# Attention beside an MLP on one core: the order of v products, dense products and scores within a unit of TensorE work

## The chip, the cores and the metric

The kernel runs on one core of one Trainium2 chip. The metric is the device time in microseconds of one execution. Before the change it is 1629.68 us, the median of three runs (1628.3 to 1630.91).

## What is computed

The reference, cut to its core (S = 2048 rows, D = 512, 32 heads of 16, F = 1792):

```python
xn = _layernorm(x)
# attention
q, k, v = heads((xn @ wqkv))                   # 32 heads, 16 wide
scores = einsum("bhqd,bhkd->bhqk", q, k) * 16 ** -0.5
o = einsum("bhqk,bhkd->bhqd", softmax(scores), v)
# MLP
h = gelu(xn @ w1 + b1)
out = x + o @ wo + (h @ w2 + b2)
```

All inputs and the output are float32.

## The kernel before, in words

Operands of the dense products and of the scores are split into two float16 parts, and a product is made of three float16 products. TensorE is used as two row halves of 64 rows, each with four column groups of 32. `tiled` (line 177) issues one product of a half as four matmuls, one for each column group, so one product fills a half. The two halves hold different work at the same time; what a half does is called its side, 0 or 1.

Three kinds of work share TensorE. The scores are made twice: as S (`s_half`, line 224, tile pS), whose row maxima VectorE takes with a reduction (line 236), and, 20 units later and transposed, as T (`e_half`, line 269, tile pT), which ScalarE turns into exponentials (line 283, tile pe) with the maxima already subtracted in the product. One S and one T stand together in the order and are called a pair here (`scores`, line 582). The products with v (`v_one`, line 299, tile pV, float32) take the exponentials of earlier units; a round is four of them, one for each head and column group. The dense products (tile pD) belong to the MLP, to the later projections of q and k, and to the output product; they come in groups (`Group`, line 394) that gather in one PSUM bank and are then evicted. A generator hands the groups over one at a time, and `dense(gen, side, n)` (line 546) issues up to n products of the current group on one side; it stops where the group has none left for that side. A group ends when both sides are done.

The order on TensorE is written out by hand in `unit` (line 562); the engines' queues keep it. One unit makes four pairs on side r (r changes from unit to unit), two rounds with v on side 1-r (`v_turn`, a generator that yields behind each round), and dense products on both sides. How many is the group's `pace`: a pair of numbers, for side 1-r and side r. The first dense product of the MLP (w1, evicted by `hidden`, 24 products a group, 14 groups to a block of 512 rows) alternates (4, 4) and (3, 3); the second (w2, 84 products a group, four groups a block) has (3, 3) in blocks 0 and 1 and (3, 4) in blocks 2 and 3; projections and output have (4, 4).

PSUM has eight banks: at any time three for S, three for T, one for the dense group and one for the products with v. A group that ends gives its bank to T's list and the next takes T's oldest. An S must wait until the reduction that read its bank has ended, a T for the exponential. Because both halves add into one bank, a v product or a dense product that changes side waits until the last one of the other side has ended (`product`, line 159).

VectorE also evicts w1's groups (line 969), ScalarE evicts w2's groups and takes the tanh (lines 984 and 939), and GpSimdE does the rest of the gelu in small steps that `tick` hands out unit by unit. DMAs are issued on SyncE.

Of the kernel before, what the change touches and what calls it, by code (L numbers as in the profile page):

```python
# [24 lines left out]
NC = D // P  # L25
# [3 lines left out]
NG = H // 4  # L29
VW = DH + 1  # L30
LEAD = 20
FAST, MEAN, SLOW = (4, 4), (3, 4), (3, 3)
MEASURE = (3, 0, 1, 2)
POOL_NS = 2500
TAIL = 5
# [11 lines left out]
def layer_kernel(ctx: ExitStack, tc: tile.TileContext, x, wqkv, wo, w1, b1, w2, b2, out):  # L47
# [104 lines left out]
    PAIRS = ((0, 0), (0, 1), (1, 0))  # L152
# [37 lines left out]
    def later(n, fn, local=False):  # L190
        queue.append((slot[0] + n, fn, local))
# [10 lines left out]
    def pooled(*todo):  # L202
        steps.extend(todo)
# [8 lines left out]
    def tick():  # L212
        run_due()
        run_steps()
        slot[0] += 1
# [8 lines left out]
    def s_half(u, n):  # L224

        t, i = divmod(u, 16)
        g, qb = divmod(t, NQB)
        qt, kb = divmod(i, 4) if t else (i % 4, i // 4)
        if t not in mt_of:
            mt_of[t] = work.tile([P, 4, 4, 4], F32, name="mt", bufs=2)  # L230
        ks, qs = kst[g % 2], qst[g % 2]
        p, a = divmod(n, 2)
        r = slice(64 * a, 64 * a + 62)
        s = banks("S")
        tiled(None, a, s, qs[p][qb][r, qt * P:(qt + 1) * P], ks[p][kb][r, :], True, True)
        nc.vector.reduce_max(mt_of[t][:, n, qt, kb:kb + 1], s, axis=AX.X)  # L236
# [283 lines left out]
    pos, spent, cur = [0], [False], [None]  # L520

    def group(gen):

        if cur[0] is None and not spent[0]:
            cur[0] = next(gen, 0)
            if cur[0] == 0:
                cur[0], spent[0] = None, True
        return cur[0]

    def ended():  # L530

        if cur[0] is not None and cur[0].over():
            done, cur[0] = cur[0], None
            newest.pop("D", None)
            done.end()

    def burst(gen, n):

        while n > 0 and (f := group(gen)) is not None:
            if not f.usable():  # L540
                break
            f.product(2)
            n -= 1
            ended()

    def dense(gen, side, n):

        while n > 0 and (f := group(gen)) is not None and f.usable(side):
            f.product(side)
            n -= 1  # L550
            ended()
# [10 lines left out]
    def unit(gen):  # L562

        u = pos[0]
        e = u - LEAD
        if e < 0:
            pos[0] += 1
            for n in range(4):  # L570
                s_half(u, n)
            s_end(u)
            burst(gen, LFILL[u - 16])
            tick()
            return
        if e == 0 and cur[0] is not None:
            burst(gen, cur[0].left())
        r = e % 2

        v = v_turn(1 - r, pos[0] - (2 if e < NU else 0))  # L580

        def scores(i):
            k, n = divmod(i, 2)
            if u - r < NU:
                s_half(u - r + k, 2 * n + r)
            if e - r < NU:
                e_half(e - r + k, 2 * n + r)

        pace = cur[0].pace if cur[0] is not None else FAST
        dense(gen, 1 - r, pace[0] - 2)  # L590
        scores(0)
        dense(gen, 1 - r, 2)
        scores(1)
        next(v, None)
        scores(2)
        next(v, None)
        scores(3)
        for _ in v:
            pass
        dense(gen, r, pace[1])  # L600
        for t in [t for t in pv_of if summed[t] == [32] * 4]:
            v_end(t)
        for key in [k for k in ptiles if not any(w[1:] == k for side in due for w in side)]:
            del ptiles[key]
        pos[0] += 1
        if u < NU and r:
            s_end(u)
        tick()
# [9 lines left out]
    with ExitStack() as st1:  # L618
# [285 lines left out]
        while not spent[0] or more or cur[0] is not None:  # L904
            unit(fil)
            if pos[0] > 16:
                more = next(pre, 0) != 0
# [3 lines left out]
    def mlp():  # L911
        m2 = st2p
        w2_s = m2.tile([P, 2, NF, D], F16, name="w2_s")
        b2_b = m2.tile([P, D], F32, name="b2_b")
        xbs, wcs = {}, {}

        def fetch_x(b):
            if b < NQB:
                xbs[b] = m2.tile([P, 2, NC, QB], F16, name="xb", bufs=1)
                nc.sync.dma_start(xbs[b], xn_d[:, :, :, b * QB:(b + 1) * QB])  # L920

        def fetch_w1(n):
            if n < NQB * NF:
                wcs[n] = m2.tile([P, 2, NC, P], F16, name="wc", bufs=3)
                nc.sync.dma_start(wcs[n], w1_d[n % NF])

        fetch_x(0)
        for n in range(2):
            fetch_w1(n)
        for _ in range(8):  # L930
            yield None

        done = set()

        def gelu(hh, g, b, f):
            t1 = m2.tile([P, QB], F32, name="t1", bufs=2)

            def tanh():
                nc.scalar.activation(t1, t1, AF.Tanh, scale=GELU_C * GELU_A)
                later(1, rest, True)  # L940

            def rest():
                pooled((690, lambda: nc.gpsimd.tensor_scalar(t1, t1, 1.0, gs[:, 1:2], op0=ALU.add, op1=ALU.mult)),
                       (1280, lambda: nc.gpsimd.tensor_tensor(t1, t1, hh, op=ALU.mult)),  # L944
                       (620, lambda: nc.gpsimd.tensor_scalar(g[:, 0, f, :], t1, 1.0, 0.0, op0=ALU.mult, op1=ALU.add)),
                       (1160, lambda: nc.gpsimd.tensor_tensor(g[:, 1, f, :], t1, g[:, 0, f, :], op=ALU.subtract)),  # L946
                       (0, lambda: done.add((b, f))))

            pooled((1040, lambda: nc.gpsimd.tensor_tensor(t1, hh, hh, op=ALU.mult)),  # L949
                   (620, lambda: nc.gpsimd.tensor_scalar(t1, t1, 1.0, 1.0 / GELU_A, op0=ALU.mult, op1=ALU.add)),  # L950
                   (1280, lambda: nc.gpsimd.tensor_tensor(t1, t1, hh, op=ALU.mult)),  # L951
                   (0, lambda: later(2, tanh, True)))

        for b in range(NQB):
            xb = xbs[b]
            g = m2.tile([P, 2, NF, QB], F16, name="g", bufs=1)
            for f in range(NF):
                fetch_w1(b * NF + f + 2)
                wc = wcs[b * NF + f]
                if b == 0 and f >= 3:  # L960
                    nc.sync.dma_start(w2_s[:, :, f - 3:NF if f == NF - 1 else f - 2, :],
                                      w2_d[:, :, f - 3:NF if f == NF - 1 else f - 2, :])
                if b == 0 and f == 3:
                    nc.sync.dma_start(b2_b, b2[None, :].to_broadcast([P, D]))

                def hidden(hp, g=g, b=b, f=f):
                    hh = m2.tile([P, QB], F32, name="hh", bufs=3)
                    scale, bias = fac1[0][:, f // 2:f // 2 + 1], b1_s[:, f:f + 1]
                    nc.vector.tensor_scalar(hh, hp, scale, bias, op0=ALU.mult, op1=ALU.add)  # L969
                    later(1, lambda: gelu(hh, g, b, f), True)  # L970

                yield Group([lambda c=c, i=i, j=j, wc=wc, xb=xb: (wc[:, i, c, :], xb[:, j, c, :])
                             for c in range(NC) for i, j in PAIRS], dbank, hidden, pace=FAST if f % 2 else SLOW)
            for q in range(4):
                t = b * 4 + q
                xa = m2.tile([P, D], F32, name="xa", bufs=2)
                if q == 1:
                    fetch_x(b + 1)
                nc.sync.dma_start(xa, x[t * P:(t + 1) * P, :])
                later(3, lambda xa=xa: pooled((1280, lambda: nc.gpsimd.tensor_tensor(xa, xa, b2_b, op=ALU.add))), True)  # L980

                def store(yp, xa=xa, t=t):
                    yt = m2.tile([P, D], F32, name="yt", bufs=2)
                    nc.scalar.activation(yt, yp, AF.Copy, scale=gs[:, 2:3])  # L984
                    add = lambda: nc.gpsimd.tensor_tensor(xa, xa, yt, op=ALU.add)  # L985
                    put = lambda: nc.sync.dma_start(acc_d[t * P:(t + 1) * P, :], xa)
                    later(1, lambda: pooled((1280, add), (0, lambda: later(1, put, True))), True)

                yield Group([lambda f=f, i=i, j=j, q=q, g=g: (g[:, i, f, q * P:(q + 1) * P], w2_s[:, j, f, :])
                             for f in range(NF) for i, j in PAIRS], dbank, store,  # L990
                            lambda n, b=b: (b, n // 3) in done, pace=SLOW if b < 2 else MEAN)
# [128 lines left out]
```

## Time and profile before

| | before |
|---|---|
| median of 3 runs | 1629.68 us (1628.3 to 1630.91) |
| the profiled execution | 1630.98 us, its span 1629.1 us |
| granted TensorE clock | 0.992 |
| TensorE busy | 97% of the span, 38915 matmuls |
| VectorE, ScalarE, GpSimdE busy | 88%, 85%, 41% |
| reductions of S (line 236) | 2048, mean 683 ns |
| exponentials (line 283) | 2048, mean 688 ns |

A line of the profile names the source line, engine and operation, the tiles written and read, the shape of one instruction and the count; then the busy time, the mean duration of one, and the idle time of that engine just before, with what ended it. All tiled products carry the line of `product` (161), so they are told apart by tile: pS, pT, pV, pD. In the timeline the first two columns are the start and the length of a row of equal instructions that follow each other. The lengths of matmuls are modelled and overlap, so the distance between starts is what a product costs.

### The profile page before, as it was taken

Reading aid. Unit: us, or ns where it says so; the run is one execution under the profiler, and the core shown is the slowest. Engines: PE = TensorE matmul, PEld = TensorE weight load, DVE = VectorE, ACT = ScalarE, POOL = GpSimd, SP = SyncE. Lnnn points to the kernel's source line nnn. Section 1 sums busy time; section 2 is a strip of 40 time slices with the busy share of each in tenths; the row PEclk is TensorE's granted clock in tenths of the full one; section 3 lists DMA queues with packets and bytes.
Section 4 is the critical chain, followed back from the end, with each engine's and each line's share of the span. In section 5 each row is a group of like instructions: output and inputs, shape, how many; then the busy total and the mean of one; then the engine's idle time right before and its main releaser. Section 6 shows DMA issues by size and latency. Waiting matters only on the chain.

```text
span 1629.1 us, 85743 instructions
## 1 busy us (share of the span) xinstructions
PE 1583.1 (97%) x38915; PEld 965.3 (59%) x38915; DVE 1425.7 (88%) x2388; ACT 1383.9 (85%) x2254; POOL 668.5 (41%) x742
## 2 busy tenths in 40 slices
PE   8987999979999999999999999999999999999998
PEld 3434666636666666666566666666666656665554
DVE  8887988869999999999999999999999989998901
ACT  4316988869999999999999999999999989998893
POOL 3112686527774110677412166761117774111000
PEclk9999999989999999999999999999999999999999
DMA  6475475451112111211111111221111100004122
GB/s 201 145 229 174 115 191 171 133 187 45 44 42 62 41 40 38 60 50 38 51 37 50 41 45 39 58 62 39 39 48 49 40 27 25 26 23 146 54 87 99
DMA packets 120934, 125.79 MB, mean 77 GB/s; under 512 B 39036, under 2 KB 90620, under 8 KB 120440
## 3 DMA queue, kind: packets, MB, share of 16 engines
q1 hardware_dynamic: 120568, 120.30, 25.2%
q8 instruction: 304, 4.98, 1.3%
q14 instruction: 62, 0.51, 0.1%
HBM read 81.79 MB, written 38.39 MB: 74 GB/s over the span
## 4 chain that ended last, share of the span: by engine, by line
PE 84%; DVE 5%; DMA 4%; POOL 3%; SPq 1%; issue 1%; ACT 1%; POOLq 0%; DVEq 0%; ACTq 0%
PE pV L161 29%; PE pD L161 26%; PE pS L161 13%; PE pT L161 11%; DVE mt L236 3%; PE pD L418 1%; DMA wch<-in_B_w_dram 1%; PE pT L418 1%; SPq L345 1%; DVE amx L634 1%; PE pT L510 1%; DMA wc<-w_d 0%; POOL osb L338 0%; DMA m_d<-mhl 0%; DMA qst<-m_d 0%
## 5 line engine op out<-in xcount | busy, mean ns | idle before, releaser
L283 ACT ACTIVATE pe<-pT,sexp 128x512 f32<-128x512 f32 x2048 | 1284.3, 688 | 124.3 <-PE pT L161 87.6
L236 DVE TENSOR_REDUCE mt<-pS 128x1 f32<-128x512 f32 x2048 | 1299.7, 683 | 99.1 <-PE pT L161 70.8
L161 PE MATMUL pV<-pe,vv 64*32 64x512 f32 x8192 | 989.6, 591 | 1.2 <-issue 1.2
L161 PE MATMUL pS<-kst,qst 62*32 62x512 f16 x8192 | 856.1, 381 | 16.5 <-DVE mt L236 15.3
L161 PE MATMUL pT<-qst,kst 64*32 64x512 f16 x8192 | 857.3, 379 | 5.6 <-DMA qst<-m_d 3.8
L161 PEld LDWEIGHTS <-qst 62*32 62x32 f16 x8192 | 326.7, 90 | 205.5 <-issue 146.9
L161 PE MATMUL pD<-xb,wc 64*32 64x512 f16 x5376 | 333.0, 377 | 11.4 <-DMA wc<-w_d 11.4
L161 PE MATMUL pD<-w_s,g 64*32 64x512 f16 x5376 | 331.5, 375 | 0.0
L161 PEld LDWEIGHTS <-kst 64*32 64x32 f16 x8192 | 282.2, 91 | 81.8 <-issue 50.8
L161 PEld LDWEIGHTS pV<-pe,vv 64*32 64x32 f32 x8192 | 276.1, 107 | 89.2 <-issue 39.7
L161 PEld LDWEIGHTS <-wc 64*32 64x32 f16 x5376 | 160.4, 92 | 92.0 <-issue 13.4
L161 PEld LDWEIGHTS <-g 64*32 64x32 f16 x5376 | 162.5, 92 | 72.0
L257 POOL TENSOR_SCALAR mhl<-msb 64x64 f16<-64x64 f32 x32 | 7.6, 237 | 285.0 <-DVE msb L255 285.0
L985 POOL TENSOR_TENSOR xa<-xa,yt 128x512 f32<-128x512 f32 x16 | 20.5, 1278 | 239.2 <-ACT yt L984 237.4
L161 PE MATMUL pD<-xt,wqk_h 64*32 64x512 f16 x1920 | 117.1, 376 | 0.0
L949 POOL TENSOR_TENSOR t<-hh 128x512 f32<-128x512 f32 x56 | 58.2, 1039 | 134.9 <-DVE hh L969 134.0
L161 PEld LDWEIGHTS <-wqk_h 64*32 64x32 f16 x1920 | 59.2, 92 | 28.6 <-issue 1.2
L951 POOL TENSOR_TENSOR t<-t,hh 128x512 f32<-128x512 f32 x56 | 71.7, 1280 | 4.7
L944 POOL TENSOR_TENSOR t<-t,hh 128x512 f32<-128x512 f32 x56 | 71.6, 1279 | 4.7
L338 POOL TENSOR_TENSOR osb<-osb,rb 128x512 f32<-128x512 f32 x31 | 39.7, 1280 | 75.4 <-DMA rb<-den_d 39.5
L946 POOL TENSOR_TENSOR g<-t,g 128x512 f16<-128x512 f32 x56 | 65.1, 1162 | 4.4
L161 PE MATMUL pD<-wo_s,oc 64*32 64x512 f16 x768 | 47.1, 376 | 0.0
(136 smaller groups left out, 877.4 us busy)
## 6 DMA issues: line engine op xcount, KB each, us to landing
wch<-in_B_w_dram SPq DMA_DIRECT2D x28, 512.0 KB
wc<-w_d SPq DMA_DIRECT2D x56, 256.0 KB
qk_d<-stg SPq DMA_DIRECT2D x32, 256.0 KB
rb<-den_d SPq DMA_DIRECT2D x124, 64.0 KB
kst<-qk_d SPq DMA_DIRECT2D x128, 48.0 KB
qst<-qk_d SPq DMA_DIRECT2D x128, 48.0 KB
xs<-in_A_x_dram SPq DMA_DIRECT2D x16, 256.0 KB
qk_d<-stg SPq DMA_DIRECT2D x32, 128.0 KB
```

The lines of the kernel that those rows point to most:

```text
L161: p = nc.tensor.matmul(*args, **kw)
L236: nc.vector.reduce_max(mt_of[t][:, n, qt, kb:kb + 1], s, axis=AX.X)
L283: ex = nc.scalar.activation(pe, st, AF.Exp, scale=sexp[:, g // 2:g // 2 + 1])
L338: pooled((1280, lambda: nc.gpsimd.tensor_tensor(osb, osb, rb, op=ALU.mult)), (620, lambda: nc.gpsimd.tensor_scalar(ot[:, 0], osb, 1.0, 0.0 ...
L345: nc.sync.dma_start(ot_d[64 * g + DH * h:64 * g + DH * h + DH, :, qb * QB:(qb + 1) * QB], ot[32 * h:32 * h + DH])
L418: nc.tensor.matmul(self.bank, lhs, rhs, start=start, stop=self.last and self.over())
L510: nc.tensor.matmul(pj, xt[:, i, c, t * P:(t + 1) * P], wh[j][:, c, :], start=(n == 0), stop=(n == 11))
L944: (1280, lambda: nc.gpsimd.tensor_tensor(t1, t1, hh, op=ALU.mult)),
L946: (1160, lambda: nc.gpsimd.tensor_tensor(g[:, 1, f, :], t1, g[:, 0, f, :], op=ALU.subtract)),
L949: pooled((1040, lambda: nc.gpsimd.tensor_tensor(t1, hh, hh, op=ALU.mult)), (620, lambda: nc.gpsimd.tensor_scalar(t1, t1, 1.0, 1.0 / GELU_A ...
L951: (1280, lambda: nc.gpsimd.tensor_tensor(t1, t1, hh, op=ALU.mult)),
L985: add = lambda: nc.gpsimd.tensor_tensor(xa, xa, yt, op=ALU.add)
```

## The change

Within a unit the order is another: a round with v comes first, then dense products on the side of the scores, the first pair, two dense products on that side, the second round with v, the other three pairs, and at the end two dense products on the side of the v products. The pace becomes one number, the dense products of a unit (8, 7 or 6, as the sums of the pairs were); the w1 groups, which alternated between 8 and 6, get 7 each.

```diff
-FAST, MEAN, SLOW = (4, 4), (3, 4), (3, 3)
+FAST, MEAN, SLOW = 8, 7, 6
...
-        pace = cur[0].pace if cur[0] is not None else FAST
-        dense(gen, 1 - r, pace[0] - 2)
+
+        next(v, None)
+        dense(gen, r, (cur[0].pace if cur[0] is not None else FAST) - 4)
         scores(0)
-        dense(gen, 1 - r, 2)
-        scores(1)
+        dense(gen, r, 2)
         next(v, None)
-        scores(2)
-        next(v, None)
-        scores(3)
+        for i in range(1, 4):
+            scores(i)
         for _ in v:
             pass
-        dense(gen, r, pace[1])
+        dense(gen, 1 - r, 2)
...
-                             for c in range(NC) for i, j in PAIRS], dbank, hidden, pace=FAST if f % 2 else SLOW)
+                             for c in range(NC) for i, j in PAIRS], dbank, hidden, pace=MEAN)
```

## The prediction

> **What bounds the kernel now.** I read the page first, then the exponentials by stage, then one unit of work in the timeline.
>
> ```profile
> span 1629.1 us, 85743 instructions
> PE 1583.1 (97%) x38915; PEld 965.3 (59%) x38915; DVE 1425.7 (88%) x2388; ACT 1383.9 (85%) x2254; POOL 668.5 (41%) x742
> PE 84%; DVE 5%; DMA 4%; POOL 3%; SPq 1%; issue 1%; ACT 1%; POOLq 0%; DVEq 0%; ACTq 0%
> L283 ACT ACTIVATE pe<-pT,sexp 128x512 f32<-128x512 f32 x2048 | 1284.3, 688 | 124.3 <-PE pT L161 87.6
> L236 DVE TENSOR_REDUCE mt<-pS 128x1 f32<-128x512 f32 x2048 | 1299.7, 683 | 99.1 <-PE pT L161 70.8
> ```
>
> TensorE carries 84% of the chain, and what idle time ScalarE and VectorE have before the exponentials (L283) and the reductions (L236) is mostly ended by TensorE. The 2048 exponentials come four to a unit, so 512 units make up the kernel after its opening. The windows give the unit's length, from the count of exponentials (columns: stretch, length, DVE, ACT, clock, DMA share, GB/s):
>
> ```profile
> 150.00:320.00 170.00, 1.16 (x2) 141.45 (x220) 1.00 0.52 152
> 506.00:640.00 134.00, 0.00 (x0) 125.04 (x205) 1.00 0.13 36
> 646.00:780.00 134.00, 0.00 (x0) 116.75 (x186) 1.00 0.18 49
> 1090.00:1200.00 110.00, 0.00 (x0) 101.09 (x162) 1.00 0.12 33
> ```
>
> Four times length over count: 3.09 us in the projections (8 dense products a unit), 2.61 in the second dense product of blocks 0 and 1 (6 a unit), 2.88 in the first dense product (8, 8, 7, 8, 6, 6, 5 in the built order, mean 6.86), 2.72 in the second of blocks 2 and 3 (7). Two units of this last kind, in the timeline:
>
> ```profile
> 1126.81 0.39 PE L161 MATMUL pD<-w_s,g 64*32 64x512 f16 x3
> ...
> 1126.85 0.60 PE L161 MATMUL pV<-pe,vv 64*32 64x512 f32 x3
> ...
> 1127.47 0.39 PE L161 MATMUL pS<-kst,qst 62*32 62x512 f16 x1
> ...
> 1127.67 0.40 PE L161 MATMUL pD<-w_s,g 64*32 64x512 f16 x4
> ...
> 1127.88 0.40 PE L161 MATMUL pD<-w_s,g 64*32 64x512 f16 x4
> ...
> 1128.32 0.61 PE L161 MATMUL pV<-pe,vv 64*32 64x512 f32 x4
> ...
> 1128.75 0.61 PE L161 MATMUL pV<-pe,vv 64*32 64x512 f32 x4
> ...
> 1129.62 0.60 PE L161 MATMUL pV<-pe,vv 64*32 64x512 f32 x3
> ...
> 1131.70 0.40 PE L161 MATMUL pS<-kst,qst 62*32 62x512 f16 x4
> ...
> 1131.91 0.40 PE L161 MATMUL pT<-qst,kst 64*32 64x512 f16 x4
> ...
> 1132.13 0.38 PE L161 MATMUL pD<-w_s,g 64*32 64x512 f16 x1
> ```
>
> and the reductions that belong to it, with ten microseconds of unhindered ones from the units without dense products:
>
> ```profile
> 1130.36 0.69 DVE L236 TENSOR_REDUCE mt<-pS 128x1 f32<-128x512 f32 x1 [0.19 <-PE pT L161]
> 1487.41 10.25 DVE L236 TENSOR_REDUCE mt<-pS 128x1 f32<-128x512 f32 x17
> ```
>
> Four readings.
> First, prices: a dense or score product (four matmuls side by side in one row half) holds its half 0.215 us (1127.67 to 1127.88), a round of four v products two passes of 0.43 (1128.32 to 1128.75), so 0.86. Reductions follow each other in (10.25-0.69)/16 = 0.598.
> Second, the halves run apart from each other: pS at 1127.47 starts before the pD of 1127.67, which stands ahead of it in the program.
> Third, results are handed over in order: the fourth score pair stands behind the second v round, whose last pass ends at 1129.62+0.43 = 1130.05, and its reduction starts only at 1130.36, 0.31 later.
> Fourth, TensorE doesn't look ahead without end: pS at 1127.47 has its half free since 1126.85+0.43 = 1127.28 and starts 0.19 later. In the order, 28 matmuls stand between that last v pass and this pS. In the units without dense products 8 stand there, and there is no such gap:
>
> ```profile
> 1491.87 0.61 PE L161 MATMUL pV<-pe,vv 64*32 64x512 f32 x4
> ...
> 1492.33 0.40 PE L161 MATMUL pS<-kst,qst 62*32 62x512 f16 x4
> ```
>
> (1491.87+0.43 = 1492.30, 0.03 before pS.) I read it as a look-ahead of about 28 matmuls past the oldest unfinished one, and 0.19 us to go on.
>
> So before, two units go round one loop: from the tail's pD at 1126.81, p dense products on one half (p a unit's number; 7 x 0.215 = 1.51), two v rounds (1.72), hand-over (0.31), the reductions of the fourth pair and of the next first pair, which frees the bank of the next fourth (0.598+0.69+0.05 = 1.34, giving 1130.05+0.31+1.34 = 1131.70: the row), that pair (0.43), and the next tail at 1132.13. Sum: 5.32 us for two units; in general 3.80+0.215p, or 1.90+0.108p a unit: 2.55 for p=6, 2.66 for 7, 2.76 for 8. Measured 2.61, 2.72, 3.09; the rest is what a finished dense group adds (eviction and what follows it), below.
>
> **The change, part by part.** Nothing is removed or added: in the built programs the matmuls are as many, and so are VectorE's, ScalarE's and GpSimdE's instructions, SyncE's DMAs, and the 511 side waits of the v products; those of the dense products go from 496 to 499, a wait each for a product several slots old, which I cost at nothing (if late, one product, 0.215, every unit: 110 us; the 12 or more products between make it unlikely). DMAs and GpSimdE steps hang on group ends and move with them by a few units; POOL is 41% busy. What moves is order. With A the half with v and B the half with scores, a unit becomes: v on A, p-4 dense on B, first pair, 2 dense on B, v on A, three pairs, 2 dense on A.
>
> The new loop on one half, from the first v round: 0.86; then the second round. Between it and the last pass of the first stand p-4 dense, a pair and 2 dense, p products or 4p matmuls: 28 for p=7, 24 for 6. So it waits the 0.19 of the fourth reading: 0.19+0.86. Then 2 dense, with three pairs, 24 matmuls, between: 0.19+0.43. Next unit, the same half as B: p-4, 2, 2 and 6 products, (p+6) x 0.215. Sum: 3.82+0.215p for two units, 1.91+0.108p for one: 0.01 us more than before. The waits of 0.19 replace the wait for the fourth pair's bank.
> The reductions make a second loop, since now three pairs stand behind the second v round: hand-over 0.31, the second, third, fourth and next first reduction 3 x 0.598+0.69, 0.05, the fourth pair 0.43, and the next v rounds 0.86+0.19+0.86: 5.18 for two units, 2.59 a unit whatever p. For p=6 that is 0.04 over before.
>
> Sum over stages. Second dense product: about 113 units at p=6, +0.04: +4; about 93 at 7, +0.01: +1. Projections and output, about 95 units at 8: +1. First dense product: a half that has run out of products leaves its places empty, and the built order gives 7, 7, 5, 7, 7, 7, 5, 7, 7, 6, 7, mean 6.55, so 56 groups of 24 products take 205 units where they took 196. By the loops a unit is 2.64 in both orders. The 9 more units come out of the units without products, 6 where there were 17, at 4 x 0.598 = 2.39 each: 205 x 2.64 - 196 x 2.64 - 11 x 2.39 + 2 x 2.66 = +3. Together +9 us, on the profiled execution's 1630.98 (span 1629.1, 1.9 around it, and 1.3 above the median of 1629.68): about 1639.
>
> What I hold equal is the cost of a finished group. Its nearest rows:
>
> ```profile
> L969 DVE TENSOR_SCALAR hh<-pD,fac,b_s 128x512 f32<-128x512 f32 x56 | 44.9, 802 | 0.8 <-PE pT L161 0.7
> L939 ACT ACTIVATE t<-t 128x512 f32<-128x512 f32 x56 | 34.8, 621 | 0.0
> ```
>
> Before, 2.88-2.64 = 0.24 a unit or 0.84 a group, close to the 0.80 of one hh: the reductions are in the loop, so each insertion counts in full. I take the same after, with nought and twice that as the ends. A new group may now start in the middle of a run and take the T bank whose exponential is oldest; with two younger ones between I cost that at nothing, at worst one exponential (0.688) for each of 56 groups, 39 us.
>
> **Rivals.**
> *The slack swallows the group's cost (faster).* Before, the reductions stand in the one loop that sets the pace; after, at p=7, their loop of 5.18 us is 0.15 short of the other (5.33), and they are busy 4 x 0.598 = 2.39 of 2.67 us, so that a late one can be made up over the next units. If each of the 56 first-product groups and about 16 projection groups gets back half of its excess (0.42 and, at 0.33 a unit over three units, 0.5), that is -24-8 = -32, and with the +9 about 1608. For it: the idle 0.19 before the reduction, once a unit, which the new order doesn't need. Against it: three pairs now come in a row, 6 x 0.215 = 1.29 us of products for 3 x 0.598 = 1.79 us of reductions, and for p=6 the reductions are the loop.
> *Semaphore waits stop the look-ahead (slower).* Each of the three pairs in a row waits for two banks, and the tail's dense products and the next v round stand behind them: a matmul that waits for its bank holds all that is queued on TensorE. If the tail starts only with the fourth pair (place p+4 on B), the next unit starts p+6.25 products after this one (two tail products and the 0.05 of a bank's release): 2.86 for p=7, 3.07 for 8, 2.64 for 6, 2.75 for 6.55. Against the measured units, with the groups' excess kept in full: 93 x 0.20 + 95 x 0.31 + 113 x 0.09 + 205 x 0.11 = +80; with none of it 93 x 0.14 - 95 x 0.02 + 113 x 0.03 - 205 x 0.13 = -12; the lost idle units add 5. I take the half between, +39: 1670. It decides where the fourth pair's bank comes later than the second v round's end plus 0.19. Against it: before, a pair that waits for its bank (1131.70) already stands ahead of each tail.
> *Strict order.* The row is pS at 1127.47 ahead of an older pD. If starts were in order, the tail on A could begin only behind the last product of B, and the next unit behind the tail's: one product a unit lost against before, 0.215 x 495 units with dense products: +106, 1737. [...]
> *The order changes nothing.* Both loops are within 0.01 us at p=7 and 8, so no difference is a case of its own.
>
> **How the numbers follow.** Forecast, slower by some 4 to 25 us: 0.41. Semaphore rival 0.20, strict order 0.02: slower 0.63. No change (within 0.2%, 3.3 us, about what a measurement here can tell): 0.10. Swallowed group cost 0.27, as the pairs' spacing does leave slack: faster 0.27. The likeliest gives 1639, its own range 1633 to 1655. To leave out no more than 2 in 10 the range takes in the faster rival's 1608 with a few microseconds for a larger share of the excess, and the semaphore rival's 1670 with some way to its own upper end: 1603 to 1683.
>
> **What would show it.** In the changed kernel's timeline at p=7: a second v round 0.19 after the first has ended; the tail's pD 0.19 after the second v round; reductions without the 0.19 idle time once a unit; units of 2.72 to 2.76 there and 2.63 to 2.70 for p=6; 6 units without products. The semaphore rival would show tails that start with the fourth pair; the faster one first-product units under 2.80. Wrong is all of it if the second v round starts at once after the first, or only after the first pair.

## The result and the profile after

The changed kernel takes 1681.61 us (median of 4 runs, 1678.35 to 1683.49) against 1630.3 (4 runs, 1628.3 to 1631.38) on the same chip: ratio 1.0314, 95% interval 1.0295 to 1.0333. It is 51 us slower where +9 was forecast.

The page of the changed kernel, the lines that answer to those shown of before:

```profile
span 1676.3 us, 85755 instructions
PE 1600.9 (96%) x38915; PEld 961.0 (57%) x38915; DVE 1416.7 (85%) x2388; ACT 1380.8 (82%) x2254; POOL 668.4 (40%) x742
PE 72%; DVE 14%; DMA 5%; POOL 3%; issue 2%; ACT 2%; SPq 2%; DVEq 0%; POOLq 0%; ACTq 0%
L283 ACT ACTIVATE pe<-pT,sexp 128x512 f32<-128x512 f32 x2048 | 1280.3, 689 | 172.1 <-PE pT L161 119.5
L236 DVE TENSOR_REDUCE mt<-pS 128x1 f32<-128x512 f32 x2048 | 1290.1, 684 | 153.3 <-PE pS L161 90.0
```

The chain now runs 14% over VectorE (5% before), yet VectorE waits longer ahead of its reductions (153.3 us, 99.1 before): engines that each wait for the other. The windows by stage, the exponentials alone (length, busy, count; four times length over count is a unit), first of the changed kernel:

```profile
169.60:326.40 156.80, 125.92 (x201) 0.99 0.54 157
515.60:634.20 118.60, 106.19 (x173) 1.00 0.13 37
682.90:800.30 117.40, 100.66 (x160) 1.00 0.17 47
1411.40:1502.90 91.50, 79.89 (x128) 1.00 0.09 25
```

and the units of its last three rows in the kernel before:

```profile
508.50:622.00 113.50, 105.82 (x172) 1.00 0.14 38
669.10:784.60 115.50, 100.81 (x160) 1.00 0.21 59
1379.50:1466.80 87.30, 79.84 (x129) 1.00 0.10 28
```

A count can hold one exponential that is cut at the window's edge. Between the starts of the same two exponentials in both traces a unit takes, with the one before in brackets: projections 3.13 us (3.11), second product at p=6 2.77 (2.64), first product 2.93 (2.89), second product at p=7 2.85 (2.73). From the means over all four blocks: about 113 units x 0.12 = 13 us, 93 x 0.125 = 12, first product 205 x 2.944 - 196 x 2.904 - 11 x 2.39 + 2 x 2.8 = 14, projections 1; the remaining 11 are put down to the output stage (two runs below take 9 to 10 of them off). There a product stands on TensorE's queue before its operand has landed (waits of the changed kernel):

```profile
PE pD L161 <- DMA oc<-ot_d: 6.4, 1, 6.4
```

That unit takes 11.4 us. No such wait is there before, where the MLP ends nine units earlier and more units without products follow it while the load is under way.

One undisturbed unit at p=7 and the start of the next two, in the timeline of the changed kernel:

```profile
1200.26 0.61 PE L161 MATMUL pV<-pe,vv 64*32 64x512 f32 x4
...
1201.34 0.65 PE L161 MATMUL pV<-pe,vv 64*32 64x512 f32 x3
...
1201.83 0.60 PE L161 MATMUL pV<-pe,vv 64*32 64x512 f32 x2
...
1202.41 0.40 PE L161 MATMUL pD<-w_s,g 64*32 64x512 f16 x4
...
1202.53 1.29 DVE L236 TENSOR_REDUCE mt<-pS 128x1 f32<-128x512 f32 x2 [0.27 <-PE pT L161]
...
1205.17 0.39 PE L161 MATMUL pD<-w_s,g 64*32 64x512 f16 x1
...
1205.68 0.59 PE L161 MATMUL pV<-pe,vv 64*32 64x512 f32 x1
```

The half comes round in 1205.68-1200.26 = 5.42 us for two units, 2.71 a unit: first to second v round 1.08, second round to tail (the two dense products at the end of a unit) 1.07, tail and 13 products 3.27. The forecast had 1.05, 1.05 and 3.23. So in this quiet unit the sum is nearly right; the units at p=7 with no other instruction of VectorE or ScalarE in or shortly before them (31 units) take 2.75 as a mean, 0.09 more than forecast. What it missed is why the tail starts when it does. A second, later unit:

```profile
1207.24 0.62 PE L161 MATMUL pV<-pe,vv 64*32 64x512 f32 x3
...
1207.95 0.40 PE L161 MATMUL pD<-w_s,g 64*32 64x512 f16 x4
1208.01 0.47 PE L161 MATMUL pS<-kst,qst 62*32 62x512 f16 x4
```

and VectorE and ScalarE beside the two tails (rows of two narrower windows):

```profile
1200.99 1.35 ACT L283 ACTIVATE pe<-pT,sexp 128x512 f32<-128x512 f32 x2
...
1206.58 1.28 DVE L236 TENSOR_REDUCE mt<-pS 128x1 f32<-128x512 f32 x2
```

The second v round ends at 1207.24+0.43 = 1207.67; the tail starts 0.28 later, 0.09 after the reduction that ends at 1207.86. That is the first pair's reduction, whose bank the fourth pair needs; the fourth pair stands ahead of the tail in TensorE's queue and holds it, although its own half is still busy until 1208.01, so no wait shows at that pair. In the unit above, the tail (1202.41, all four matmuls at once) follows the exponential that ends at 1202.34 by 0.07. Taken over the trace (start of the tail against the end of the first pair's reduction and exponential in the same unit), the tail starts less than 0.22 us, mostly 0.07 to 0.14, behind the later of the two in 94 of 100 units at p=7 and in the first product, in 89 at p=6.

### The profile page after: what moved, and what is told of

It reads as the page before. It is cut to its first block, busy times and chain, and to the rows that moved or that the text cites. A ratio compares the mean times of both kernels' runs of the same rounds, so it can differ in the third digit from the quotient of the medians.

```text
span 1676.3 us, 85755 instructions
## 1 busy us (share of the span) xinstructions
PE 1600.9 (96%) x38915; PEld 961.0 (57%) x38915; DVE 1416.7 (85%) x2388; ACT 1380.8 (82%) x2254; POOL 668.4 (40%) x742
## 4 chain that ended last, share of the span: by engine, by line
PE 72%; DVE 14%; DMA 5%; POOL 3%; issue 2%; ACT 2%; SPq 2%; DVEq 0%; POOLq 0%; ACTq 0%
PE pV L161 25%; PE pD L161 16%; PE pS L161 14%; PE pT L161 13%; DVE mt L236 11%; ACT pe L283 2%; DVE hh L968 2%; PE pD L418 1%; DMA wch<-in_B_w_dram 1%; PE pT L418 1%; PE pT L510 1%; DMA wc<-w_d 0%; DMA dn<-den_d 0%; DMA out_dram<-ac 0%; DVE amx L633 0%
## 5 line engine op out<-in xcount | busy, mean ns | idle before, releaser
L236 DVE TENSOR_REDUCE mt<-pS 128x1 f32<-128x512 f32 x2048 | 1290.1, 684 | 153.3 <-PE pS L161 90.0
L161 PE MATMUL pV<-pe,vv 64*32 64x512 f32 x8192 | 1105.0, 596 | 0.0
L161 PE MATMUL pS<-kst,qst 62*32 62x512 f16 x8192 | 818.8, 379 | 37.2 <-DVE mt L236 32.1
L161 PE MATMUL pT<-qst,kst 64*32 64x512 f16 x8192 | 823.1, 378 | 4.6 <-DMA qst<-m_d 3.6
L161 PEld LDWEIGHTS <-qst 62*32 62x32 f16 x8192 | 281.2, 92 | 267.1 <-issue 120.2
L161 PE MATMUL pD<-xb,wc 64*32 64x512 f16 x5376 | 371.6, 378 | 14.8 <-DMA kst<-qk_d 11.5
L161 PE MATMUL pD<-w_s,g 64*32 64x512 f16 x5376 | 376.2, 377 | 0.0
L161 PEld LDWEIGHTS <-kst 64*32 64x32 f16 x8192 | 259.1, 93 | 148.9 <-issue 16.1
L161 PEld LDWEIGHTS <-wc 64*32 64x32 f16 x5376 | 140.6, 91 | 70.7 <-issue 29.1
L161 PEld LDWEIGHTS <-g 64*32 64x32 f16 x5376 | 143.4, 91 | 38.4 <-issue 5.1
L161 PE MATMUL pD<-xt,wqk_h 64*32 64x512 f16 x1920 | 130.3, 380 | 0.0
```

The costliest lines, as they stand in the source:

```text
L161: p = nc.tensor.matmul(*args, **kw)
```

## The experiments

Times are medians; the ratio is to the kernel before, run on the same chip beside it. Differences in the text go by the ratios, times 1630 us (the changed kernel: 1.0314).

| run | us | ratio (95%) |
|---|---|---|
| before, pace of the w1 groups even | 1636.7 | 1.0023 (1.0011 to 1.0035) |
| changed, old pace | 1675.7 | 1.0260 (1.0242 to 1.0278) |
| changed, output held back | 1675.1 | 1.0255 (1.0232 to 1.0278) |
| changed, second pair ahead of the second v round | 1641.9 | 1.0053 (1.0033 to 1.0073) |
| changed, second v round earlier | 1701.9 | 1.0423 (1.0396 to 1.0449) |
| before, one reduction more a group | 1670.1 | 1.0232 (1.0202 to 1.0262) |
| changed, the same | 1719.7 | 1.0534 (1.0509 to 1.0558) |
| second pair ahead, the same | 1675.2 | 1.0257 (1.0230 to 1.0283) |
| changed, half reductions | 1649.2 | 1.0100 (1.0085 to 1.0115) |
| before, half reductions | 1590.3 | 0.9740 (0.9725 to 0.9755) |
| changed, tail ahead of the fourth pair | 1661.6 | 1.0185 (1.0158 to 1.0212) |
| changed, half reductions and exponentials | 1616.6 | 0.9913 (0.9891 to 0.9935) |
| before, dense sides exchanged | 1838.1 | 1.1273 (1.1250 to 1.1296) |
| drawn version | 1604.3 | 0.9823 (0.9808 to 0.9838) |
| drawn version, first pair in front | 1617.7 | 0.9926 (0.9897 to 0.9955) |
| drawn version, old pace | 1597.2 | 0.9792 (0.9772 to 0.9813) |

From the starts of the matmuls in each trace, the idle time of a half between two products, as a mean for one unit and both halves together, in us. A unit loses half of it, since each half comes round in two units. "v to v" is the idle time ahead of the second v round, "v to tail" that ahead of the tail, "all" the whole. By where a stage is cut, a value moves by up to 0.05:

| kernel | p=6: v to v, v to tail, all | p=7: v to v, v to tail, all | first product, all |
|---|---|---|---|
| before | -, -, 0.50 | -, -, 0.51 | 0.86 |
| changed | 0.16, 0.38, 0.73 | 0.25, 0.32, 0.71 | 0.99 |
| second pair ahead | 0.29, 0.12, 0.50 | 0.34, 0.12, 0.54 | 0.78 |
| second v round earlier | 0, 0.53, 0.91 | 0.05, 0.56, 0.83 | 1.06 |
| half reductions | 0.17, 0.35, 0.62 | 0.24, 0.28, 0.60 | 0.84 |
| half reductions and exponentials | 0.16, 0.17, 0.49 | 0.26, 0.18, 0.54 | 0.66 |
| tail ahead of the fourth pair | 0.16, 0.03, 0.69 | 0.25, 0.02, 0.57 | 0.91 |
| drawn version, old pace | 0.24, 0, 0.38 | 0.27, 0, 0.34 | 0.59 |

All, at p=6: 0.73-0.50 is 0.23, half of it 0.115, and a unit there lost 0.12. Before, the idle time lies elsewhere: 0.16 (p=6) and 0.24 (p=7) ahead of the first pair, which stands behind the other unit's v round, and 0.15 and 0.12 ahead of the fourth.

**The pace, and the output stage.**

```diff
-                ... hidden, pace=FAST if f % 2 else SLOW)
+                ... hidden, pace=MEAN)
```

> The kernel before with one part of the change alone: every w1 group gets (3, 4), 7 products a unit, in place of (4, 4) and (3, 3) in turn. The order within a unit stays. Theory one (the pace costs only by the units it adds: 11 units of first product, 2.88 each, in place of 11 units without products, 2.39 each, some of the 5 us back because the mean p falls from 6.86 to 6.55): within 4 us of the kernel before, about 1632. Theory two (the MLP that ends later leaves too few units to cover the loading of the output product, the 11.4 us stall of the changed kernel's unit 498): plus 8 to 12, about 1640, with that stall in the trace.

Theory one: 1636.7, 3.7 above the kernel before by the ratio. The stall is there (10.5 us at the same unit), as theory two had it, but the first product gains: 2.85 a unit against 2.90.

The changed kernel with that line undone:

```diff
-                ... hidden, pace=MEAN)
+                ... hidden, pace=FAST if f % 2 else SLOW)
```

> The changed kernel with the pace of the w1 groups undone: 8 and 6 in turn instead of 7. The order within a unit stays the new one. Theory one (the pace is harmless by itself, the order costs all 51 us): 1682 within 4 us. Theory two (the pace shortens the stretch without products and so uncovers the load of the output product): 11 to 13 us less, about 1670, no stall over 5 us at the first output group.

9 us less, nearer to theory two; the stalled unit shrinks from 11.4 to 5.5 us.

```diff
-                while qb not in blocks or pos[0] < min(blocks[qb][1] + 2, NU + LEAD):
+                while qb not in blocks or pos[0] < min(blocks[qb][1] + 6, NU + LEAD):
```

> The changed kernel with the first output groups held back: an output block is used 6 units after its load is issued instead of 2. Order and pace stay the new ones. If the 11.4 us stall at the first output product is TensorE's queue standing behind a product whose operand has not landed, 8 to 10 us less (four more units without products at 2.4 to 2.8 each run in the same time), about 1673. If the time only moves to another wait (the later one on the stacked queries, or products left over after the last unit), 1682 within 3 us.

The stall is gone, and 10 us with it. Either run takes off about 9 of the 51 us; the order keeps 42.

**Three pairs in a row.**

```diff
         dense(gen, r, 2)
+        scores(1)
         next(v, None)
-        for i in range(1, 4):
+        for i in range(2, 4):
             scores(i)
```

> The changed kernel with one pair moved: the second score pair stands ahead of the second round with v, so that two pairs follow that round and not three. The rest is the changed kernel. Theory one (three pairs in a row behind a v round bunch the reductions: VectorE gets four results late together and the loss of a late reduction is not made up): units come down to the ones before, 2.75 at p=7 and 2.66 at p=6, first product 2.89: 410 units of the MLP by 0.05 to 0.10, 20 to 35 us less, about 1655. Theory two (the gaps of 0.19 behind both v rounds, which the look-ahead sets, are what can't be made up): one gap of two is only moved, since 9 products instead of 7 stand between the two v rounds: no gain, 1682 or up to 10 more.

One pair moved gives back 43 us: units of 2.65 at p=6 and 2.83 in the first product. What is left over before, 8.6 us, is about what the output stage costs, and the stall is still there (a unit of 12.5 us). So the loss of the order is the second pair's place. The tail's gap falls from 0.38 to 0.12; the gap between the v rounds grows by 0.1 as theory two said, and is outweighed. A quiet tail of this kernel:

```profile
1383.85 0.63 PE L161 MATMUL pV<-pe,vv 64*32 64x512 f32 x4
1384.35 0.40 PE L161 MATMUL pD<-w_s,g 64*32 64x512 f16 x4
...
1384.68 0.39 PE L161 MATMUL pS<-kst,qst 62*32 62x512 f16 x4
```

It starts at 1384.35, 0.07 after 1383.85+0.43, with 16 matmuls between, and ahead of the fourth pair (1384.68), which is older.

**The gap between the v rounds.**

```diff
         scores(0)
-        dense(gen, r, 2)
         next(v, None)
+        dense(gen, r, 2)
```

> The changed kernel with the second round with v put two dense products earlier: it follows the first pair at once, and the two dense products that stood between them come behind it. Between the two rounds stand 5 products (20 matmuls) at p=7 instead of 7 (28); three pairs still follow the second round. Theory one (the loop of the reductions, 5.18 us for two units with a fourth pair that needs the bank of the first, leaves no room for a late one): that loop is as long as before, so 1682 within 8 us, the units at 2.7 to 2.9. Theory two (the 0.19 us that the look-ahead costs at each second round): that gap goes, 0.095 a unit over some 490 units, 35 to 45 us less, about 1642.

Both theories fall: 18 us slower. The gap between the rounds does go (0.05 and 0), but the tail, now with 32 matmuls between, waits 0.53 to 0.56. The 32 matmuls alone account for about half of that (0.27 to 0.29, by the medians at the end); the rest is again the first pair's banks, since a v round that ends earlier leaves the tail a longer wait for the same release: it starts less than 0.22 us behind it in 96 of 100 units at p=6 and 67 at p=7. The gap taken from one place came back at the next.

**The cost of a finished group.** In all three kernels, behind the eviction:

```diff
+                    nc.vector.reduce_max(spare, hh, axis=AX.X)
```

> The kernel before with one instruction added to each finished w1 group: a reduction of hh over its 512 columns on VectorE, right behind the eviction, into a spare column that nothing reads (56 of them, an estimated 0.6 to 0.69 each from the reductions of the scores, so some 36 us of VectorE in all). The prediction's term (the reductions are in the loop that sets the pace, so an insertion counts in full): plus 34 to 39. Rival (the old order has slack and makes part of it up): plus 10 to 25.

> The changed kernel with the same added instruction as in the run on the kernel before, 56 reductions of hh on VectorE behind the evictions of the w1 groups. Theory one (three pairs in a row: the loop of reductions is nearly as long as TensorE's, so that a late reduction is not made up): plus 32 to 40 over the changed kernel, about 1717, and more than the kernel before pays for the same. Theory two (the cost of a finished group is equal in both orders, as the prediction held it): the same plus as in the kernel before, within 5 us.

> The changed kernel with the second pair ahead of the second round with v (1642 by its own run), and the same added instruction as in the two runs beside it. Theory one (with two pairs behind the v round the loop of reductions is one reduction shorter, 4.58 us for two units instead of 5.18, and absorbs a late one): plus 5 to 20, clearly less than the changed kernel pays. Theory two (what the earlier pair brings has nothing to do with slack for VectorE): plus 32 to 40 as the changed kernel.

The added instruction, in the groups of the kernel before with it:

```profile
L971 DVE TENSOR_REDUCE spare<-hh 128x1 f32<-128x512 f32 x56 | 38.4, 686 | 1.9
```

38.4 us of VectorE cost 38 us before, 36 in the changed order, 33 with the second pair ahead, each within about 5 us. The prediction's term holds in each: what VectorE inserts counts nearly in full, and equally within the intervals. That the new order makes up less of a late reduction is refuted, and so is the 5 to 20 us expected with the second pair ahead.

**What holds the tail.**

```diff
-        nc.vector.reduce_max(mt_of[t][:, n, qt, kb:kb + 1], s, axis=AX.X)
+        nc.vector.reduce_max(mt_of[t][:, n, qt, kb:kb + 1], s[:, 0:QB // 2], axis=AX.X)
```

> The changed kernel with reductions over 256 columns in place of 512, an estimated 0.35 to 0.4 us each instead of 0.69 (half of the keys of each block are left out of the row maxima). Banks for the pairs are then never late. Theory one (what the new order costs over 1.91 + 0.108 p a unit are waits for the banks that the reductions free, the fourth pair's above all, with the tail queued behind it): the tail starts 0.19 or less after the second v round instead of 0.27 to 0.29 on average, no tail starts with the fourth pair, units 2.67 to 2.72 at p=7, 2.57 to 2.62 at p=6, first product 2.62 to 2.70: 90 to 115 us less, about 1580. Theory two (the gaps of the look-ahead, which don't depend on the reductions): the tail's gaps stay as they are, only the cost of what VectorE inserts goes: 40 to 60 us less, about 1630.

> The kernel before with reductions over 256 columns in place of 512 (half of the keys of each block are left out of the row maxima), for comparison with the same in the changed order. By the prediction's reading (before, the wait for the fourth pair's bank, 1.34 of the 5.32 us of two units, sets the pace, and the halves are occupied for 4.95 us of them at p=7): units fall to between 2.47 and 2.58 at p=7, 80 to 130 us less in all, about 1530. If the old order is set by TensorE's own queue and not by the reductions: under 40 us less.

The page of the changed kernel with half reductions:

```profile
L236 DVE TENSOR_REDUCE mt<-pS 128x1 f32<-128x256 f32 x2048 | 784.6, 420 | 584.1 <-PE pS L161 300.3
```

A reduction takes 420 ns instead of 684. The changed kernel gains 35 us, where neither theory stood (90 to 115, 40 to 60). The kernel before gains 42, half of the least that the prediction's reading promised there (80 to 130): the wait for the fourth pair's bank is real but small. By the starts in the trace the fourth pair's S is late by 0.18 us a unit in the kernel before, nearly always until just behind the end of a reduction. With half reductions it is late by 0.02, but then the T of the pair is late by 0.08, in half of the units until just behind the end of an exponential. In the changed kernel the tail's gap stays at 0.28 to 0.35, which looked like theory two; but in the trace of the changed kernel with half reductions the tail now starts mostly 0.07 to 0.13 behind the exponential of the first pair, in nine of ten units less than 0.22, where the reduction had been the later one in 61 of the 100 held units at p=6. The one holder had only given way to the other. So both were shortened:

```diff
-        ex = nc.scalar.activation(pe, st, AF.Exp, scale=...)
+        ex = nc.scalar.activation(pe[:, 0:QB // 2], st[:, 0:QB // 2], AF.Exp, scale=...)
```

> The changed kernel with reductions and exponentials both over 256 columns in place of 512 (half of the keys are left out of the row maxima, and half of each exponential tile stays at 1, set once at the start, which may lengthen the opening by up to 20 us; the units of the stages are what tells). Theory one (the tail is held by the release of the first pair's banks, which the fourth pair ahead of it needs): the tail's gap behind the second v round falls from 0.28 to 0.39 with halved reductions alone to about 0.15, as v rounds with 24 matmuls between show it; clean units from 2.72 to 2.69 at p=7 and from 2.58 to 2.54 at p=6; first product from 2.87 to under 2.75; 1649 less 30 to 50, without a longer opening. Theory two (the gap is the look-ahead's own, larger for dense products than for v products): the gap stays at 0.28 or more, units as with the reductions alone, 1649 within 10.

Its page, and a tail at p=7 in its timeline:

```profile
L285 ACT ACTIVATE pe<-pT,sexp 128x256 f32<-128x256 f32 x2048 | 874.8, 473 | 491.3 <-PE pT L161 407.2
```

```profile
1374.43 0.61 PE L161 MATMUL pV<-pe,vv 64*32 64x512 f32 x2
1374.87 0.39 PE L161 MATMUL pD<-w_s,g 64*32 64x512 f16 x1
1375.01 0.40 PE L161 MATMUL pD<-w_s,g 64*32 64x512 f16 x3
```

Theory one: another 31 us, and the tail's mean gap is 0.17 to 0.18 (0.24 in the first product); three of its matmuls start 0.15 behind 1374.43+0.43 = 1374.86, the first at once. At p=7 the tail stands within 0.22 us of a release in 10 of 100 units, where it was 94; at p=6 it is 0.13 to 0.21 behind one, twice what a held tail is. The unit times expected were nearly reached: 2.78 in the first product, where under 2.75 was expected; 2.76 at p=7 and 2.61 at p=6 in the units that hold no eviction, and 2.71 and 2.55 in those that have none in the 3 us before them either, where 2.69 and 2.54 were expected.

The tail moved instead:

```diff
-        for i in range(1, 4):
+        for i in range(1, 3):
             scores(i)
         for _ in v:
             pass
         dense(gen, 1 - r, 2)
+        scores(3)
```

> The changed kernel with the tail (two dense products on the side of the v products) one pair earlier: ahead of the fourth pair instead of behind it. Three pairs still follow the second v round on their half. Theory one (the tail is held on TensorE's queue by the fourth pair, which waits for its bank, in 26 to 50 of 100 units): the tail's mean gap behind the second v round falls from 0.27 to 0.45 us to under 0.2, half of it a unit: 20 to 45 us less, about 1650. Theory two (the row of three pairs makes the reductions late, and where the tail stands doesn't matter): 1682 within 6 us.

21 us back, the lower end of theory one. The tail's gap is gone, but the fourth pair waits for its bank as long as before, and now the next unit's first dense products stand behind it: they wait 0.14 to 0.23 a unit, where it was 0.04.

**The dense products' side alone, in the old order.**

```diff
-        dense(gen, 1 - r, pace[0] - 2)
+        dense(gen, r, sum(pace) - 4)
         scores(0)
-        dense(gen, 1 - r, 2)
+        dense(gen, r, 2)
...
-        dense(gen, r, pace[1])
+        dense(gen, 1 - r, 2)
```

> The kernel before with one part of the change alone: the dense products change sides (p-4 and 2 on the side of the scores, the last 2 on that of the v products), while the v rounds stay behind the second and third pair. If the place of the first v round matters (9 products of the other half, 36 matmuls, then stand ahead of it in the queue, and TensorE was seen to look ahead without a gap only some 20): the v half waits about 0.3 us more in each unit, 1700 to 1790. If only the tail behind the fourth pair matters: about 1670.

1838: dearer than expected. The first v round has no dense products of its own half ahead of it. Between it and the pair that its half made last stand 10 products of the other half at p=6 and 11 at p=7, two more than the expectation counted, since the tail ahead of them belongs to the same half; its half idles 1.35 us a unit with 10, 1.57 with 11, 1.78 with 12. In this order the exchange of sides needs the v round in front.

**A version from the runs.** The body of a unit becomes

```python
next(v, None)
dense(gen, r, pace - 5)
scores(0)
dense(gen, r, 2)
scores(1)
next(v, None)
scores(2)
for _ in v:
    pass
dense(gen, 1 - r, 3)
scores(3)
```

with `pace` read ahead of it (the current group's, or FAST), and output groups held back by 6 units.

> A version drawn from what the runs show: second pair ahead of the second v round, the tail ahead of the fourth pair and of three products instead of two (p-5 instead of p-4 in front), and output groups held back by 6 units. If the waits of the v side (0.4 to 0.6 us a unit between its first v round and its tail) are what both orders lose, they nearly vanish and a unit comes near its occupied 2.47 us at p=7: 30 to 70 us below the kernel before, about 1580. If the fourth pair, now last on TensorE's queue, delays the next unit's v round and dense products instead: 1630 to 1650.

The same with the first pair in front:

```diff
         next(v, None)
+        scores(0)
         dense(gen, r, pace - 5)
-        scores(0)
-        dense(gen, r, 2)
         scores(1)
+        dense(gen, r, 2)
         next(v, None)
```

> The version at 1604 us with the first pair moved to the front: v round, first pair, p-5 dense, second pair, two dense, v round, third pair, three dense on the v side, fourth pair. The first pair's banks come free about 0.4 to 0.6 us earlier, so the fourth pair is late less often (0.12 us a unit in the first product now); but the fourth pair of one unit and the first of the next now follow each other. If the fourth pair's bank is what is left: 5 to 20 us below 1604. If the bunching weighs more: 1604 to 1620.

And the first of the two with the old pace (`FAST if f % 2 else SLOW`) for the w1 groups:

> The version at 1604 us with the pace of the w1 groups as it was before, 8 and 6 in turn instead of 7. The changed kernel gained 6 us from that and the kernel before lost 4 by the even pace. If the MLP that ends 9 units earlier is worth as much here: 1598 within 3. If the even pace saves as much in the units as it adds in their number: 1604 within 3.

1604, 29 us under the kernel before and so just short of the 30 to 70 expected, and 1597 with the old pace of the w1 groups, as its first theory had it: 2.1% under the kernel before. The tail's gap is nought, with 8 matmuls between, and the chain is TensorE's again:

```profile
PE 82%; DVE 7%; DMA 4%; POOL 3%; issue 2%; SPq 1%; ACT 1%; DVEq 0%; POOLq 0%; ACTq 0%
L236 DVE TENSOR_REDUCE mt<-pS 128x1 f32<-128x512 f32 x2048 | 1272.5, 683 | 75.8 <-PE pT L161 47.9
```

The first pair in front costs 17 us by the ratios (13 by the medians), so the bunching weighs more: that pair then waits 0.07 to 0.16 a unit.

## Why the prediction was wrong

**The price of the tail's wait failed.** The step "then 2 dense on A, with three pairs, 24 matmuls, between: 0.19+0.43" took only the gap seen behind 28 matmuls, and in the sum of the stages the second dense product then cost 5 us and the first 3, where 25 and 14 were measured. The tail's wait, measured as a mean, is 0.38 at p=6, 0.32 at p=7, 0.47 in the first product. With reductions and exponentials halved 0.17 (p=6) and 0.18 (p=7) are left, 0.24 in the first product; v rounds with 24 matmuls between wait 0.15. The rest, by this estimate, is the fourth pair's bank. That the quiet unit shown comes near the forecast (0.15 where 0.19 stood) is partly luck: there too the tail follows a release, by 0.07. The prediction had both halves of this, in separate places. It had the loop of reductions, but led it to the next v round, where it was 0.15 short of TensorE's at p=7 and so cost nothing; it had the tail behind the pairs, but as a rival with the chance 0.20. Joined: from the end of a second v round, hand-over 0.31, four reductions 3 x 0.598+0.69 = 2.48, and 0.09 to the tail, 2.88. By the rows shown, 1202.26 (1201.83+0.43) + 2.88 = 1205.14 against the row 1205.17. The two holders run side by side and end within 0.06 of each other, the reductions at 1205.05, the exponentials at 1205.11 (rows of a wider window):

```profile
1202.53 2.52 DVE L236 TENSOR_REDUCE mt<-pS 128x1 f32<-128x512 f32 x4 [0.27 <-PE pT L161]
1202.59 2.52 ACT L283 ACTIVATE pe<-pT,sexp 128x512 f32<-128x512 f32 x4 [0.24 <-PE pT L161]
```

One unit is 2.64 to 2.71, so the tail comes 0.17 to 0.24 after its own v round even if nothing disturbs it, and what VectorE inserts adds to that: the 38.4 us of added reductions cost 36 in this order. With the second pair ahead there is one reduction less, 2.28: under a unit, and the gap falls to 0.12.

**The bank of a new group was costed at nothing, and is not nothing.** The waits of the changed kernel have a row of which the kernel before has none:

```profile
PE pD L161 <- ACT pe L283: 3.0, 12, 0.4
```

It holds only the waits in which all of TensorE stood still. By the starts in the traces the first dense product of 26 of the 56 w1 groups and of 10 of the 16 w2 groups waits more than 0.05 us for its bank while its half is free, most of them until 0.05 to 0.1 us behind the end of an exponential; before, one w1 group did. Together these are 18 us of one half's time, without one long wait for a load in the first block that both kernels have. No run shows what this alone adds to the kernel's time.

**The semaphore rival was the true mechanism, at a smaller price per unit than its upper end.** Its premise, that a waiting matmul holds what is queued behind it, shows at the output product, where TensorE idles 6.4 us for one product's operand, and in the tails, which follow the first pair's release by less than 0.22 us in 94 of 100 units at p=7. Its time of 1670 is 12 us short; 9 of them are the output stage, which it did not have. Its sign, tails that start with the fourth pair, shows in half of the units at p=6 and a quarter at p=7 (within 0.06 us); the better sign is the release, since the pair itself often waits for its half a little longer.

**Right:** the second v round's wait (0.15 at 24 matmuls, 0.235 at 28; forecast 0.19 for both); the loop of before (quiet units at p=7 are long and short in turn, 5.31 to 5.34 for two, where 5.32 was summed), though the reductions are not its only holder; the loop of after within 0.1 us of 5.33 in the unit shown; that starts run out of order between the halves (the tail of 1384.35 ahead of the older pS of 1384.68); six units without products. The rival of strict order falls with the row of 1384.35.

**The equal cost of a finished group** was right for what VectorE inserts, by the added reductions; for the bank of the next group it was not. The faster rival (slack swallows it) falls with that.

**Not foreseen:** the load of the output product. The step "DMAs and GpSimdE steps hang on group ends and move with them by a few units" overlooked what hid the load, the units without products between the stages, which the same step cut from 17 to 6. It cost about 9 us.

**By the signs named:** units of 2.72 to 2.76 at p=7 and 2.63 to 2.70 at p=6 were wrong (2.86 and 2.76 as means over both stretches); the reductions' idle time once a unit, expected to go, stays (0.27 in the row at 1202.53).

## What to carry to other kernels

The order on TensorE's queue joined two loops that looked separate: the tail, which stood behind a pair that waited for its banks, started less than 0.22 us, mostly 0.07 to 0.14, behind the later of their releases in 94 of 100 units at p=7, even where the pair's own half was still busy and no wait showed at it. Ahead of that pair its gap fell from 0.38 and 0.32 us to 0.03 and 0.02. Sum the loop through the step that is held, not only to the step that waits, and ask for every buffer which step must have released it and what that one stands behind. When shortening one holder changes nothing, look who holds next before calling it innocent.

## What was not expected of the hardware

The wait behind a v round goes with the number of matmuls of the other half that stand between. As a mean over the four matmuls of the product that waits, the medians over the traces of eight kernels, for v rounds and score pairs, are: none at 8 and 16, 0.045 us at 20, 0.15 at 24, 0.235 at 28, 0.27 to 0.29 at 32, 0.31 at 36. The prediction read a limit of about 28 and a fixed 0.19 out of rows with 28 and 8 between; that was an estimate, and no run shows such a limit or what in TensorE sets these waits. The mean climbs steadily, but a single matmul's wait comes in a step: at 20 three of the four start at once and one 0.18 late, at 24 one at once and three about 0.19 late (0.15 in the rows at 1374.87 and 1375.01), at 28 all four 0.22 to 0.24 late. In the run with the dense sides exchanged, where a v round waits behind a pair of its own half, 40, 44 and 48 matmuls cost 1.35, 1.57 and 1.78: there each product more (four matmuls) adds 0.22 and 0.21, where a product holds its half 0.215.
